# Moving a spatial product and a projection behind attention as three-part products, and input products into attention

## The chip, the core and the metric

The kernel runs on one core of one Trainium2 chip. Its engines work on queues of their own and meet at semaphores: TensorE (PE) for matrix products, with weight loads (PEld) that overlap them, the vector engine (DVE), the scalar engine (ACT), GpSimd (POOL) and SyncE (SP), which issues most DMAs. The metric is the device time of one execution in microseconds; lower is better.

## The reference

Three layers follow one another, for 2 batches of 576 positions, 8 heads of 64, model width 512:

```python
# 1. attention that keeps the 32 largest scores of each row
scores = scale * q @ k.T
kth    = 32nd largest of each row
attn   = softmax(where(scores >= kth, scores, -1e9))
x      = concat_heads(attn @ v)
# 2. gated MLP with a product over positions ("spatial")
h      = gelu(x @ w_in);  u, v = halves of h           # 512 columns each
v_n    = layernorm(v) * g_ln
v_s    = einsum('ts,bsd->btd', w_sg, v_n) + b_sg       # spatial product
x      = x + (u * v_s) @ w_out                         # projection
# 3. routed experts, one of 8 for each token
e      = argmax(x @ w_gate), or the expert of the token before if x @ w_local >= 0
out    = softmax(x @ w_gate)[e] * (relu(x @ w1[e]) @ w2[e])
```

## The kernel before

Positions are cut into tiles of 128; a batch has four whole tiles (j = 0 to 3) and one of 64 (j = 4), and the two 64s share the tile `BOTH`. Attention runs in 72 units. A unit is one head of one whole tile, or two heads of a half tile: scores (L325), copy to `s_sb` (L328), a search for the 32nd largest in eight segments (L354 to L371), sign and exponential (L365, L367), a mask (L378 to L381), five transposes (L393), copy `pt` (L396), product with v (L401). After four units the rows are divided into `row` (L406 to L417). Batch 0 takes its tiles in the order 0, 1, 2, 3, 4; batch 1 as 4, 0, 1, 2, 3. So `BOTH` is complete early in batch 1.

All other work is cut into steps that wait in a list, `between`. After each unit `pump` gives a credit of 2.0 to 2.4 us (`RATE`, L26) and takes steps off the list while the credit lasts; what is left when attention ends follows by itself. In program order the list holds:

- `load_mlp`: w_in in eight pieces (each two vector, two scalar and one GpSimd instruction, `from_double`), and w_sg;
- for each complete tile its `mlp_in`: x @ w_in in 16 products of 128 and 4 of 512 columns (L453, L459), GELU (L466, L468), layernorm, and `logits_x` (L566);
- once `BOTH` is queued: `spread(0)`, the first batch's spatial product, 40 products of 288 columns (L541); `load_projection` (w_out, and w_out times the router weights); `tail(0)`, which holds the first batch's logits and route (`decide`) and its projection, 16 products of 512 columns (L617);
- after attention `spread(1)` and `tail(1)`: logits, route, count, and the projection of batch 1 and of `BOTH`.

A plain product of float32 operands is issued as two instructions in the trace. In batch 1 the late products are written otherwise: each operand is split into a rounded half and a rest (`in_two`, an ACT copy and a subtraction on GpSimd or the vector engine), and `product` adds three instructions, high by high, high by rest, rest by high (L523). `parts` prepares the splits when `spread(1)` starts.

The order on each engine is made when the program is built, by a scheduler that follows priorities (`high_priority`) and fixed pairs (`issue_after`). The tiles that hold splits are taken from attention's rings of buffers (`s_sb` 7, `e_sb` 5, `q` or `qh` 3, `kk` 8, `v1` 2), so they also wait for units to be done.

After the last projection the rows are in DRAM (`xrows`). The addresses `frm` come from small products (L901), and 30 products of ones (L1017) keep TensorE at work until the gather (L926) brings the rows; the experts follow (L995, L1006), eight in a row.

Of the kernel before, what the change touches and what calls it, by code (L numbers as in the profile page):

```python
# [30 lines left out]
PLAIN = (True, True)  # L31

# [5 lines left out]
FILL = (2, 2, 2, 3)  # L38
# [6 lines left out]
def tile_topk_gmlp_moe(  # L45
# [123 lines left out]
    def attention(fast):  # L169
# [39 lines left out]
        def load_sg():  # L209
            nc.sync.dma_start(w_sg_sb[:, :NJ - 1, :], w_sgT[:(NJ - 1) * P].rearrange("(c p) t -> p c t", p=P))  # L210
            load_last(0)
# [34 lines left out]
        KK, QH, QL, V1, XB, XT, VN, UT, LG, DONE = {}, {}, {}, {}, {}, {}, {}, {}, {}, []  # L246

        def load_k(b, h):
            if PLAIN[b]:
                if h % 2 == 0:  # L250
                    KK[b, h] = kv.tile([P, S], F32R, name="kk", bufs=8).bitcast(F32)
                    nc.sync.dma_start(KK[b, h], kT[b, h:h + 2].rearrange("h d s -> (h d) s"))
                return
            kr = raw.tile([P, S], F32, name="kr")
            for s in range(2):
                nc.sync.dma_start(kr[s * D:(s + 1) * D], kT[b, h])
            KK[b, h] = kv.tile([P, S], F32R, name="kk", bufs=8)
            nc.scalar.activation(KK[b, h], kr, AF.Copy)
            nc.gpsimd.tensor_tensor(KK[b, h][D:], kr[D:], KK[b, h][D:].bitcast(F32), op=OP.subtract)
# [12 lines left out]
        def load_q(b, j, g):  # L272

            if PLAIN[b]:

                src = qT[b, g:g + 4].rearrange("(a h) d s -> (h d) a s", h=2)
                qr = kv.tile([P, 4, P], F32R, name="qh", bufs=3).bitcast(F32)
                if j < NJ - 1:
                    for s in range(2):
                        at = slice(s * D, (s + 1) * D)  # L280
                        nc.gpsimd.memset(qr[at, 1 - s::2, :], 0.0)
                        nc.sync.dma_start(qr[at, s::2, :], src[at, :, j * P:(j + 1) * P])
                    for h in range(4):
                        QH[b, j, g + h] = qr[:, h, :]
                    return
                nc.gpsimd.memset(qr[:, :2, :], 0.0)
                for s in range(2):
                    nc.sync.dma_start(qr[s * D:(s + 1) * D, :2, s * LAST:(s + 1) * LAST],
                                      src[s * D:(s + 1) * D, :, (NJ - 1) * P:])
                for a in range(2):  # L290
                    QH[b, j, g + 2 * a] = qr[:, a, :]
                return
            src = qT[b, g:g + 4].rearrange("h d s -> d h s")
            qr = raw.tile([P, 4, P], F32, name="qraw")
            if j < NJ - 1:
                for s in range(2):
                    nc.sync.dma_start(qr[s * D:(s + 1) * D], src[:, :, j * P:(j + 1) * P])
            else:
                nc.gpsimd.memset(qr, 0.0)
                for s in range(2):  # L300
                    for a in range(2):
                        nc.sync.dma_start(qr[s * D:(s + 1) * D, a::2, a * LAST:(a + 1) * LAST],
                                          src[:, a::2, (NJ - 1) * P:])
            qh = kv.tile([P, 4, P], F32R, name="qh", bufs=3)
            nc.scalar.activation(qh, qr, AF.Copy)
            ql = kv.tile([P, 4, P], F32R, name="ql", bufs=3)
            nc.gpsimd.tensor_tensor(ql, qr, qh.bitcast(F32), op=OP.subtract)
            for h in range(4):
                QH[b, j, g + h], QL[b, j, g + h] = qh[:, h, :], ql[:, h, :]
# [5 lines left out]
        def scores(b, j, i):  # L315

            s_ps = ps_s.tile([P, 2, 512], F32, name="s_ps")
            if PLAIN[b]:
                terms = [(QH[b, j, i], KK[b, i - i % 2]) if j < NJ - 1 else (QH[b, j, 2 * i], KK[b, 2 * i])]
            else:  # L320
                hs = [i] if j < NJ - 1 else [2 * i, 2 * i + 1]
                terms = [(w[b, j, h], KK[b, h]) for h in hs for w in (QH, QL)]
            for m, (w, k) in enumerate(terms):
                for n in range(2):
                    nc.tensor.matmul(s_ps[:, n, :HS], w, k[:, n * HS:(n + 1) * HS],  # L325
                                     start=m == 0, stop=m == len(terms) - 1)
# [115 lines left out]
        def mlp_in(t):  # L442
# [3 lines left out]
            def u(f):  # L446
                if f == 0:
                    if j == 0 or t == BOTH:
                        VN[b] = one.tile([P, 1 if t == BOTH else NJ - 1, F2], F32, name="vn2" if t == BOTH else "vn")
                        UT[b] = one.tile([P, CF, P if t == BOTH else FULL], F32, name="ut2" if t == BOTH else "ut")  # L450
# [32 lines left out]
        SG, VN2, UT2, OUT2, ORT2 = [], {}, {}, [], []  # L483
# [8 lines left out]

        def parts():
# [665 lines left out]
```

## Time and profile before

| | |
|---|---|
| three timed runs | 583.7, 582.37, 582.16 us; median 582.37 |
| the profiled execution | 582.34 us, of which the span in the trace is 580.5 |
| TensorE clock granted | 0.985 of full speed on average, 1.00 from 80 us to the last 40 |
| busy over the span | PE 90%, DVE 58%, ACT 51%, POOL 44% |
| attention, first unit's copy to last `pt` | 8.7 to 354 us |
| split products behind attention | 373.2 to 410.5 us |
| first gather for the experts | 414.6 us |

A share over the span mixes stretches with different limits: the experts (from 418 us) are TensorE and weight loads from DRAM alone, attention uses four engines. What a move is worth is read from the stretch that it leaves and the one that it enters. In the views below a product's duration runs from its issue to its modelled end; products overlap, so the pace is the distance of two starts.

### The profile page before, as it was taken

To read this page: it belongs to the slowest core of one execution; us is meant where nothing else is said; L and a number is where in the kernel's file an instruction comes from. 1 tells how busy PE (TensorE), PEld (TensorE's weight loads), DVE (VectorE), ACT (ScalarE), POOL (GpSimd) and SP (SyncE) were. 2 spreads that over 40 slices of the span, in tenths; PEclk is the share of its full clock that TensorE was granted. 3 is DMA by queue.
4 is the path that set the end of the run, shared out by engine and by line. 5 is a ranking of instruction groups with operands and counts; after the bars stand their busy time and mean duration, and the time that the engine had idled before them with its cause. 6 is when DMAs were issued, how large, how long until landed. Compare 5 with 4: busy or idle time off the path is not lost. (4 is left out here: it accounts for less than half of the span.)

```text
span 580.5 us, 10259 instructions
## 1 busy us (share of the span) xinstructions
PE 521.7 (90%) x3414; PEld 442.7 (76%) x3414; DVE 335.2 (58%) x1626; ACT 297.0 (51%) x545; POOL 258.0 (44%) x382
## 2 busy tenths in 40 slices
PE   6566898989989799998999999989889999999993
PEld 3445686867868587887866787786579999999992
DVE  4789998969789798689998711266301111111110
ACT  3579888979787887479877432321010111011110
POOL 5497997657758475447676510520310101000010
PEclk9799899999999999999999999999999999999997
DMA  8962320000000000003101300002599997684000
GB/s 173 268 191 81 112 72 5 25 1 28 20 10 28 19 16 5 11 20 92 46 29 36 110 20 19 0 1 74 186 356 387 389 376 264 234 297 169 18 36 17
DMA packets 42609, 61.55 MB, mean 106 GB/s; under 512 B 14056, under 2 KB 18152, under 8 KB 42544
## 3 DMA queue, kind: packets, MB, share of 16 engines
q1 hardware_dynamic: 40880, 55.80, 29.5%
q0 software_dynamic: 1664, 4.97, 2.5%
q8 instruction: 30, 0.49, 0.4%
q14 instruction: 35, 0.29, 0.2%
HBM read 53.68 MB, written 7.33 MB: 105 GB/s over the span
## 5 line engine op out<-in xcount | busy, mean ns | idle before, releaser
L401 PE MATMUL pv<-v,pt 128*128 128x128 f32 (+1 forms) x720 | 104.7, 279 | 7.3 <-DVE row L417 4.8
L401 PEld LDWEIGHTS pv<-v,pt 128*128 128x128 f32 x720 | 96.2, 194 | 15.1 <-DVE row L417 5.5
L369 POOL TENSOR_TENSOR rest<-s_sb,sg 128x576 f32<-128x576 f32 x72 | 93.3, 1296 | 28.5 <-ACT sg L365 27.2
L325 PE MATMUL s_ps<-kk,qh 128*128 128x288 f32 x288 | 86.2, 423 | 16.0 <-ACT s_sb L328 15.0
L354 DVE MAX8 cand<-s_sb 128x8 f32<-128x72 f32 x576 | 88.7, 219 | 13.7 <-ACT s_sb L328 13.5
L393 PE MATMUL pt_ps<-ident,e_sb 128*128 128x128 f32 x360 | 68.1, 277 | 16.3 <-ACT pt L396 5.5
L995 PE MATMUL h_ps<-xw,w_sb 128*128 128x152 f32 (+6 forms) x512 | 76.5, 298 | 1.0 <-DMA w_sb<-in_w_dram 1.0
L1006 PE MATMUL y_ps<-hT,w_sb 128*128 128x152 f32 (+6 forms) x512 | 75.3, 299 | 0.9 <-DMA w_sb<-in_w_dram 0.9
L325 PEld LDWEIGHTS s_ps<-kk,qh 128*128 128x128 f32 x288 | 50.2, 194 | 31.3 <-ACT s_sb L328 21.4
L995 PEld LDWEIGHTS h_ps<-xw,w_sb 128*128 128x128 f32 x512 | 71.4, 190 | 1.3 <-ACT hT L998 1.3
L1006 PEld LDWEIGHTS y_ps<-hT,w_sb 128*128 128x128 f32 x512 | 71.0, 190 | 1.2 <-DMA w_sb<-in_w_dram 1.2
L396 ACT ACTIVATE pt<-pt_ps 128x640 f32<-128x640 f32 x72 | 50.3, 699 | 36.3 <-PE pt_ps L393 36.1
L998 ACT ACTIVATE hT<-h_ps 128x152 f32<-128x152 f32 (+6 forms) x32 | 9.7, 302 | 113.1 <-PE h_ps L995 109.9
L393 PEld LDWEIGHTS pt_ps<-ident,e_sb 128*128 128x128 f32 x360 | 45.2, 143 | 28.2 <-ACT pt L396 8.3
L365 ACT ACTIVATE sg<-s_sb,last 128x576 bf16<-128x576 f32 x72 | 55.6, 773 | 18.7 <-DVE last L357 15.4
L371 DVE MAX8 next<-rest 128x8 f32<-128x583 f32 x72 | 54.7, 759 | 8.2 <-POOL rest L370 8.0
L367 ACT ACTIVATE e_sb<-s_sb,nm 128x576 f32<-128x576 f32 x72 | 55.5, 772 | 1.9 <-POOL nm L362 1.7
L967 POOL DMA_INDIRECT out_dram<-orow,to x10 | 10.0, 999 | 103.1 <-ACT orow L966 48.3
L328 ACT ACTIVATE s_sb<-s_ps 128x576 f32<-128x576 f32 x72 | 46.3, 642 | 13.3 <-PE s_ps L325 12.8
L1000 DVE TENSOR_SCALAR hT<-h_ps 128x152 f32<-128x152 f32 (+6 forms) x32 | 10.3, 323 | 73.6 <-PE h_ps L995 68.6
L379 POOL TENSOR_TENSOR e_sb<-e_sb,mask 128x576 f32<-128x576 f32 x36 | 46.3, 1287 | 13.4 <-ACT e_sb L367 6.7
L1008 DVE COPY yT<-y_ps 128x152 f32<-128x152 f32 (+6 forms) x32 | 9.9, 323 | 64.2 <-PE y_ps L1006 64.2
(247 smaller groups left out, 827.2 us busy)
## 6 DMA issues: line engine op xcount, KB each, us to landing
w_sb<-in_w_dram SPq DMA_DIRECT2D x32, 1024.0 KB, 12.4
dbl<-in_w_in_dram SPq DMA_DIRECT2D x8, 512.0 KB, 4.5
kk<-in_kT_dram SPq DMA_DIRECT2D x8, 288.0 KB, 4.9
qh<-in_qT_dram SPq DMA_DIRECT2D x32, 64.0 KB, 2.4
v<-in_v_dram SPq DMA_DIRECT2D x8, 256.0 KB, 6.1
dbl<-in_w_out_dram SPq DMA_DIRECT2D x4, 512.0 KB, 3.7
xin<-row SPq DMA_DIRECT2D x8, 256.0 KB, 2.0
back<-xin SPq DMA_DIRECT2D x8, 256.0 KB, 2.6
```

What stands on the lines that cost most here:

```text
L325: nc.tensor.matmul(s_ps[:, n, :HS], w, k[:, n * HS:(n + 1) * HS], start=m == 0, stop=m == len(terms) - 1)
L328: EVACS.append(nc.scalar.activation(s_sb.rearrange("p (n s) -> p n s", n=2), s_ps[:, :, :HS], AF.Copy))
L354: nc.vector.max(cand[:, 8 * g:8 * g + 8], s_sb[:, g * w:(g + 1) * w])
L365: nc.scalar.activation(sg, s_sb, AF.Sign, bias=last8[:, un, 7:8], scale=-LESS, accum_out=cnt)
L367: nc.scalar.activation(e_sb, s_sb, AF.Exp, bias=nm, scale=scale)
L369: nc.gpsimd.tensor_tensor(below[:, :S], s_sb, sg, op=OP.mult)
L371: nc.vector.max(next8[:, un, :], below)
L393: tr = nc.tensor.transpose(pt_ps[:, t * P:(t + 1) * P], p_sb[:, k0:k0 + P], ident)
L396: nc.scalar.activation(pt.rearrange("p t q -> p (t q)"), pt_ps[:, :NJ * P], AF.Relu)
L401: nc.tensor.matmul(PV[b][:, i % g, :], pt[:, t, :], V1[b][:, t, w * i * (D + 1):w * i * (D + 1) + nv], start=t == 0, stop=t == NJ - 1)
L995: nc.tensor.matmul(hp[:, :W], w1_sb[:, c, f * P:(f + 1) * P], xw[:, c, at], start=c == 0, stop=c == CD - 1)
L1006: nc.tensor.matmul(yp[:, :W], w2_sb[:, f, c * P:(c + 1) * P], hT[:, f, :W], start=f == 0, stop=f == CE - 1)
```

## The change

- `spread(0)` and the projection of batch 0 leave the list within attention. The list now holds `load_projection` right after `BOTH`, then the `mlp_in` of batch 1's tiles as they complete. After attention one list follows: `spread(0)`, logits and route of batch 0, `spread(1)`, logits, route and count of batch 1, and the projection of all nine tiles, `BOTH` last.
- `spread(0)`, the first logits and the projection of batch 0 are split products too: three instructions for each, on splits of w_sg, `vn`, `u` and w_out.
- The splits are prepared in three calls: `parts` (w_sg, `vn` of batch 0; subtractions of `vn` on the vector engine), `parts_late` (`vn` of batch 1), `parts_out` (w_out). The last 64 rows of w_sg for batch 1 go to a buffer of their own, loaded by `load_last`.
- `vn` and `ut` get a buffer for each batch; the `kk` ring has 6 instead of 8; a path that was not used (`PLAIN` false) is taken out.

```diff
-FILL = (2, 2, 2, 3)
+FILL = ((3, 5, 4), (2, 4, 3, 3))
...
-        def load_last(b):
+        def load_last(w, b):
             half = [slice(a * LAST, (a + 1) * LAST) for a in range(2)]
-            nc.gpsimd.memset(w_sg_sb[half[1 - b], NJ - 1, :], 0.0)
-            nc.sync.dma_start(w_sg_sb[half[b], NJ - 1, :], w_sgT[FULL:])
+            nc.gpsimd.memset(w[half[1 - b]], 0.0)
+            nc.sync.dma_start(w[half[b]], w_sgT[FULL:])
...
+        def split_spatial():
+            for j, hi in enumerate(of_values(S)):
+                SG[0, j] = SG[1, j] = (hi, of_scores())
+
         def parts():
...
+            split_spatial()
+            last = of_rest()
+            load_last(last, 1)
+            SG[1, NJ - 1] = (of_rest().bitcast(F32R), of_rest().bitcast(F32R))
+            rooms = [of_scores, of_scores] + [of_weights] * 5 + [of_queries] * 3
+            for j in SPREAD[0]:
+                VN2[j if j == NJ - 1 else (0, j)] = hi, lo = rooms.pop(0)()[:, :F2], rooms.pop(0)()[:, :F2]
+                in_two((hi, lo), vn_of(0, j), nc.vector)
+                in_two(SG[0, j], w_sg_sb[:, j], nc.gpsimd)
+            in_two(SG[1, NJ - 1], last, nc.gpsimd)
...
+        def parts_late():
+            sg = wts.tile([P, NJ, S], F32, name="w_sg_sb").bitcast(F32R)
+            rooms = of_values(F2) + [sg[:, j, :F2] for j in range(NJ)]
+            for j in SPREAD[1]:
+                if j < NJ - 1:
+                    VN2[1, j] = (rooms.pop(0), rooms.pop(0))
+                    in_two(VN2[1, j], vn_of(1, j), nc.gpsimd)
+            rooms += [kv.tile([P, S], F32, name="kk", bufs=6).bitcast(F32R)[:, :F2] for _ in range(6)]
+            for f in range(CF):
+                UT2[1, f] = (rooms.pop(0), rooms.pop(0))
+
+        def parts_out():
+            rooms = [of_weights] * 5 + [of_queries] * 3
+            for f in range(CF):
+                OUT2.append((rooms.pop(0)(), rooms.pop(0)()))
+                in_two(OUT2[f], w_out_sb[:, f], nc.gpsimd)
...
-                if b == B - 1:
-                    if j == js[0] and f == 0 and n == 0:
-                        parts()
-                    product(ps[0], part(VN2[j], slice(None), slice(f * P, (f + 1) * P)), part(SG[j], slice(None), at),
-                            j == js[0], j == js[-1])
-                else:
-                    nc.tensor.matmul(ps[0], vn_of(b, j)[:, f * P:(f + 1) * P], w_sg_sb[:, j, at], start=j == js[0],
-                                     stop=j == js[-1])
+                if j == js[0] and f == 0 and n == 0:
+                    (parts, parts_late)[b]()
+                if b == B - 1 and f == 1 and n == 0 and j == js[0]:
+                    parts_out()
+                vn = VN2[j if j == NJ - 1 else (b, j)]
+                product(ps[0], part(vn, slice(None), slice(f * P, (f + 1) * P)), part(SG[b, j], slice(None), at),
+                        j == js[0], j == js[-1])
...
-                else:
-                    nc.tensor.matmul(ps[0], u, w_out_sb[:, f, :], start=f == 0, stop=f == CF - 1)
+                product(ps[0], w, OUT2[f], f == 0, f == CF - 1)
...
+            steps = [step for t in [(b, j) for b in range(B) for j in range(NJ - 1)] + [BOTH] for step in project(t)]
+            return spread(0) + [(4.4, partial(decide, 0))] + spread(1) + [(4.4, partial(finish, 1, steps))]
...
                 if j == NJ - 1 and b == B - 1:
-                    between.extend(spread(0))
                     between.extend(load_projection())
-                    between.extend(tail(0))
             if b == B - 1:
-                between.extend(spread(b))
-                between.extend(tail(b))
+                between.extend(tail())
```

How the built order moves is shown at three places. A row is one instruction or several alike (xN), with its line, output and inputs; line numbers of the change are its own (scores L289, transposes L357, product with v L365, `mlp_in` L418 and L424, `logits_x` L564).

TensorE early in batch 1, before the change, where `mlp_in` of `BOTH` ends (L566):

```order
L566 MATMUL m_ps<-w_rt_sb,xT 128x90 x2
L541 MATMUL m_ps<-w_sg_sb,vn 128x288 x6
L401 MATMUL pv<-v_1852,pt 128x128
L393 MATMUL pt_ps<-ident,e_sb 128x128
L401 MATMUL pv<-v_1852,pt 128x128
L393 MATMUL pt_ps<-ident,e_sb 128x128
```

The same place with the change:

```order
L564 MATMUL m_ps<-w_rt_sb,xT 128x90 x3
L357 MATMUL pt_ps<-ident,e_sb 128x128 x5
L289 MATMUL s_ps<-kk,q 128x288 x2
L357 MATMUL pt_ps<-ident,e_sb 128x128 x5
L365 MATMUL pv<-v_1852,pt 128x128 x10
L289 MATMUL s_ps<-kk,q 128x288 x2
L365 MATMUL pv<-v_1852,pt 128x128 x5
L357 MATMUL pt_ps<-ident,e_sb 128x128 x5
L289 MATMUL s_ps<-kk,q 128x288 x2
L230 MATMUL m_ps<-ident,w_out_sb 128x128 x4
```

The products of `spread(0)` are gone from here, and three units pass before `load_projection` (L230) gives TensorE something else. At this point 54 units have their scores and 45 are transposed, in both orders.

TensorE at the end of attention, with the change (L403 transposes `row`):

```order
L365 MATMUL pv<-v_1852,pt 128x128 x9
L403 MATMUL m_ps<-ident,row 128x128 x2
L418 MATMUL m_ps<-xT,w_in_sb 128x128 x16
L424 MATMUL m_ps<-w_in_sb,xT 128x512 x4
L564 MATMUL m_ps<-w_rt_sb,xT 128x90 x4
L523 MATMUL m_ps<-v_4461,s_sb 128x288
```

The last tile's `mlp_in` directly follows the last product with v, and the first split spatial product (L523) follows it; before, the same `mlp_in` stood behind two others.

The vector engine at the hand-over to the experts, before (`back` is the last projection's sum, L620):

```order
L887 TENSOR_TENSOR slot_at_h<-iota_c,slot_h 128x100
L620 TENSOR_TENSOR back<-m_ps,back 128x512
L897 TENSOR_TENSOR idf_at<-slot_at_h,tokid 128x200
L897 TENSOR_TENSOR pslot_at<-slot_at_h,pparts 128x300
L620 TENSOR_TENSOR back<-m_ps,back 128x512
L903 TENSOR_REDUCE idf<-a_ps 128x10
```

and with the change (the sum is L610):

```order
L868 TENSOR_TENSOR slot_at_h<-iota_c,slot_h 128x100
L610 TENSOR_TENSOR back<-m_ps,back 128x512
L878 TENSOR_TENSOR idf_at<-slot_at_h,tokid 128x200
L878 TENSOR_TENSOR pslot_at<-slot_at_h,pparts 128x300
L884 TENSOR_REDUCE idf<-a_ps 128x10
```

The last sum moved ahead of `idf_at`. On TensorE the 20 products that read `idf_at` and `pslot_at` stood ahead of all 30 products of ones; with the change 20 of the 30 (L998) stand ahead of them (L882) and 10 behind.

## Rows read from the trace of the kernel before

**Rows 1.** Stretches: busy us (instructions) of each engine, clock, DMA.
```profile
core 0: us, PE busy (x) PEld busy (x) DVE busy (x) ACT busy (x) POOL busy (x), PEclk, DMA share, GB/s
98.60:176.20 77.60, 69.52 (x460) 57.61 (x459) 65.38 (x345) 65.35 (x115) 51.14 (x79) 1.00 0.07 20
227.00:373.20 146.20, 142.72 (x884) 113.26 (x883) 99.40 (x442) 88.42 (x157) 73.38 (x93) 1.00 0.11 38
260.00:300.00 40.00, 36.93 (x256) 30.86 (x255) 37.72 (x188) 35.51 (x67) 28.95 (x40) 1.00 0.17 54
373.20:410.50 37.30, 35.27 (x228) 29.44 (x227) 23.95 (x94) 6.77 (x17) 6.79 (x6) 1.00 0.12 37
```

**Rows 2.** TensorE in order of time: start us, us, engine, line, instruction.
```profile
227.16 3.11 PE L541 MATMUL m_ps<-w_sg_sb,vn 128*128 128x288 f32 x12
...
232.74 4.53 PE L541 MATMUL m_ps<-w_sg_sb,vn 128*128 128x288 f32 x18
237.11 0.49 PE L393 MATMUL pt_ps<-ident,e_sb 128*128 128x128 f32 x3
...
364.36 3.73 PE L453 MATMUL m_ps<-xT,w_in_sb 128*128 128x128 f32 x32
...
371.36 2.04 PE L566 MATMUL m_ps<-w_rt_sb,xT 128*128 128x90 f32 x16
373.19 0.38 PE L523 MATMUL m_ps<-s_sb,e_sb 128*128 128x288 f32 x1
...
381.01 0.40 PE L523 MATMUL m_ps<-s_sb,e_sb 128*128 128x288 f32 x1 [1.64 <-DVE ut L551]
...
391.03 0.40 PE L523 MATMUL m_ps<-kk,ort_h 128*9 128x512 f32 x1
...
394.18 0.47 PE L523 MATMUL m_ps<-kk 128*128 128x512 f32 x1
...
404.92 0.40 PE L523 MATMUL m_ps<-kk 128*128 128x512 f32 x1
...
410.49 0.41 PE L901 MATMUL a_ps<-idf_at,slot_at_l 128*128 128x20 bf16 x10
...
411.43 6.63 PE L1017 MATMUL y_ps<-slot_at_l,ones 128*128 128x512 bf16 x30 [0.27 <-DVE back L620]
```

**Rows 3.** Vector engine and GpSimd in order of time, at the hand-over.
```profile
410.68 0.69 DVE L620 TENSOR_TENSOR back<-m_ps,back 128x512 f32<-128x512 f32 x1 [0.87 <-PE m_ps L523]
...
411.50 0.17 DVE L919 TENSOR_SCALAR frm<-idf 128x10 int32<-128x10 f32 x1
...
414.55 1.24 POOL L926 DMA_INDIRECT xr<-xrows,frm  x1 [3.33 <-issue]
```

**Rows 4.** TensorE by line, 227 to 373: busy us, mean ns, idle before.
```profile
L541 PE MATMUL m_ps<-w_sg_sb,vn 128*128 128x288 f32 x80 | 20.6, 406 | 0.0
...
L617 PE MATMUL m_ps<-w_out_sb,ut 128*128 128x512 f32 x32 | 15.0, 602 | 0.0
...
L587 PE MATMUL m_ps<-ut,w_ort_sb 128*9 128x512 f32 x8 | 3.8, 593 | 0.0
...
L587 PE MATMUL m_ps<-ut,w_ort_sb 128*9 128x64 f32 x8 | 0.8, 220 | 0.0
```

**Rows 5.** By line over the span: the division and the copy.
```profile
L417 DVE TENSOR_TENSOR row<-pv,rc 128x256 f32<-128x256 f32 x16 | 6.6, 413 | 0.1
...
L440 ACT ACTIVATE xT<-m_ps 128x512 f32<-128x512 f32 x9 | 5.4, 599 | 5.8 <-PE m_ps L439 5.8
```

**Rows 6.** Scalar engine by line, 227 to 410.5.
```profile
L396 ACT ACTIVATE pt<-pt_ps 128x640 f32<-128x640 f32 x27 | 18.9, 699 | 29.2 <-PE pt_ps L393 29.2
...
L490 ACT ACTIVATE s_sb<-w_sg_sb 128x576 fp32r<-128x576 f32 x5 | 3.2, 677 | 0.4 <-DVE e_sb L381 0.4
```

**Rows 7.** Scalar engine in order of time: GELU of tiles 1 and 3, batch 0.
```profile
125.07 0.60 ACT L466 ACTIVATE row<-m_ps 128x512 f32<-128x512 f32 x1
...
193.79 0.60 ACT L466 ACTIVATE row<-m_ps 128x512 f32<-128x512 f32 x1
```

More of the change, by code (lines that the diff above doesn't have):

```diff
@@ L272, in load_q @@
         def load_q(b, j, g):
[L274 to L292, printed above, removed]
@@ L298, in load_q @@
             else:
-                nc.gpsimd.memset(qr, 0.0)
+                nc.gpsimd.memset(q[:, :2, :], 0.0)
                 for s in range(2):
[L301 to L306, printed above, removed]
@@ L317, in scores @@
             s_ps = ps_s.tile([P, 2, 512], F32, name="s_ps")
-            if PLAIN[b]:
-                terms = [(QH[b, j, i], KK[b, i - i % 2]) if j < NJ - 1 else (QH[b, j, 2 * i], KK[b, 2 * i])]
-            else:
[L321 to L326, printed above, removed]
+            h, pair = (i, i - i % 2) if j < NJ - 1 else (2 * i, 2 * i)
+            for n in range(2):
+                nc.tensor.matmul(s_ps[:, n, :HS], QH[b, j, h], KK[b, pair][:, n * HS:(n + 1) * HS], start=True,
+                                 stop=True)
             s_sb = wk.tile([P, S], F32, name="s_sb", bufs=7)
@@ new lines, in of_scores, with of_weights, of_rest, of_queries @@
+        def of_scores():
+            return wk.tile([P, S], F32, name="s_sb", bufs=7).bitcast(F32R)
+        def of_weights():
+            return wk.tile([P, S], F32, name="e_sb", bufs=5).bitcast(F32R)[:, :F2]
+        def of_rest():
+            return wk.tile([P, S + ADD], F32, name="rest", bufs=3)[:, :S]
+        def of_queries():
+            return kv.tile([P, 4, P], F32, name="q", bufs=3).bitcast(F32R).rearrange("p h q -> p (h q)")
+        def of_values(n):
+            room = kv.tile([P, NJ, V1[0].shape[2]], F32, name="v1").bitcast(F32R).rearrange("p j n -> p (j n)")
+            return [room[:, k * n:(k + 1) * n] for k in range(NJ)]
@@ L582, in logits @@
                 for c in range(CF):
[L583 to L588 removed]
+                    x = part(UT2[b, c], slice(None), at) if n > LAST else part(UT2[BOTH], slice(None), c, both)
+                    lm = product(ps[:E + 1, :n], part(ORT2, slice(None), c), x, c == 0, c == CF - 1)
                 ORDER.append(lm)
@@ L688, in count, with tail @@
             ORDER.append(mm)
-        def tail(b):
-            tiles = [(b, j) for j in range(NJ - 1)]
-            if b == B - 1:
-                tiles.insert(2, BOTH)
-            steps = [step for t in tiles for step in project(t)]
-            if b < B - 1:
-                return [(4.4, partial(decide, b))] + steps
-            return [(4.4, partial(finish, b, steps))]
+        def tail():
+            steps = [step for t in [(b, j) for b in range(B) for j in range(NJ - 1)] + [BOTH] for step in project(t)]
+            return spread(0) + [(4.4, partial(decide, 0))] + spread(1) + [(4.4, partial(finish, 1, steps))]
         def decide(b):
@@ L701, in spare @@
                 return ps_m.tile(shape, F32, name="m_ps")
-            if b < B - 1:
-                load_last(b + 1)
-            fills = list(FILL)
+            fills = list(FILL[b])
             def fill():
```

87 lines of the change are left out of this document (28 added, 59 removed).

## The prediction, made before the change was run

> **What bounds the kernel now.** I read the stretches first. From 227 to 373 us, where the second batch's attention runs and the first batch's late work is mixed in, TensorE is busy 142.7 of 146.2 us (97.6%), the vector engine 99.4 and the scalar engine 88.4 [rows 1]. In the first batch, where only `mlp_in` is mixed in (98.6 to 176.2 us), all three lie closer together: TensorE 89.6%, vector and scalar engine 84% each [rows 1]. So attention itself has no single bound; TensorE becomes one when it is given more. From 373 to 410.5 us, behind attention, TensorE does nearly everything (35.3 of 37.3 us; the scalar engine 6.8), and the last projection ends at 410.49 [rows 1, 2]. Then the rows of x go to DRAM, are gathered at 414.55 [rows 3], and the experts follow. I take the experts to be unchanged: what they cost is set by when the gather starts. So the sum is made at two marks: the last projection (E, 410.5 now) and the gather (E + 4.1 now).
>
> **What leaves attention.** `spread(0)` at L541 (20.6 us busy), the first batch's projection at L617 (15.0) and its logits at L587 (3.8 + 0.8): 40.2 us [rows 4]. 142.7 − 40.2 = 102.5 us of TensorE work stay ahead of the tail. The four `mlp_in` of the second batch are in that number on both sides, since already now they stand ahead of `spread(1)`; the change only moves three of them from the end of attention, where they fill it, into its middle.
>
> **How long those 102.5 us take.** The last `mlp_in`, of tile (1, 3), can't start before attention's last unit. It takes 7.0 us for its products (364.36 to 371.36) and half of 2.04 for its logits: 8.0 [rows 2]. Ahead of it lies a chain in which TensorE has nothing to do, since no step stands there in the new order: division, `row` (0.41), transposes, the copy `xT` (0.60) [rows 5], and, ahead of that copy on the scalar engine, three splits of `vn`. I put this at 2.2 us, an estimate from the two durations (1.0 together) and as much for the short steps and hand-overs; bounds 1 and 3.
> The other 94.5 us run beside 27 units of attention [rows 6]. Now TensorE waits 3.5 us in this stretch. With so much filler gone it will wait more. Two rows show how much: where weights are loaded and little else fills (260 to 300) its share is 92.3%, beside `mlp_in` 89.6% [rows 1]. Some 8 of the 27 units will run beside `load_projection`, 19 beside `mlp_in`: 90.4% on average, so 94.5 / 0.904 = 104.5 us. The ends: 97.6% as now (96.8 us), and the first batch's pace of two tiles of eight units in 68.7 us [rows 7], 27 × 4.29 = 115.9 us.
> One cost is moved earlier: the five splits of `w_sg` on the scalar engine (3.2 us now, late in attention, where it waits 29 us for transposes [rows 6]) stand, after, in one row in the first batch's attention, ahead of the fourth tile's GELU. Between 0 and 3.2; I take 1.5, since the engine is busy 84% there. The splits of `w_out` go the other way and lie beside the second spatial product; I count them at nothing, covered by its 16 us of TensorE time.
> The spatial product (0) can then start at 227.2 + 104.5 + 1.5 + 2.2 + 8.0 = 343.4 us; `spread(1)` starts at 373.19 now [rows 2].
>
> **What is added behind attention.** A split product of 288 columns is issued each 0.1336 us (75 from 381.01 to 391.03), one of 512 each 0.232 (24 from 404.92 to 410.49) [rows 2]. So 120 of the first are 16.0 us, 48 of the second 11.1, the 24 products of the first logits 3.2 (391.03 to 394.18), and the small transposes of the first batch's route about 1: 31.3. Gone is the wait of 1.64 ahead of 381.01, which came from a late `vn` of tile (1, 3). Tail: 37.3 + 31.3 − 1.6 = 67.0 us; E = 343.4 + 67.0 = 410.4, that is 0.1 earlier than now. The three-part form saves little: the 80 passes at L541 are issued each 0.243 us (18 from 232.74 to 237.11) [rows 2], 19.4 us against 16.0. The vector engine must drain two spreads in a row with a route inside the second; it is busy 24.0 of 37.3 us there now [rows 1], so I take no wait for it and keep 2 us for the range. The new `load_last` and its memset, the longer row of `back` loads on SP and the smaller `kk` ring have slack of several units or of a 2.8 us tile, and are taken at nothing; if a `kk` load is late after all, the start of the second batch slips with it.
> The Trainium skill's page "FP8 and Floating Point Precision" (TensorE Precision Notes) says that a true FP32 product is four passes through the array. Three of four would make the 19.4 us 14.6. The rows give 16.0, so the saving is 17% and not 25%; by the page the spatial term, and with it the forecast, would be 1.4 us lower.
>
> **The hand-over to the experts.** In the new order of TensorE 20 of the 30 idle products stand ahead of the small products that give `frm`, the gather's addresses; now all 30 stand behind them. And `idf_at` on the vector engine stands behind the last `back`, now ahead of it. An idle product is 0.22 us (6.63 for 30) and they start when the last `back` is done, E + 0.9 now (410.68 + 0.69) [rows 2, 3]. So `frm` is ready at E + 0.9 + 4.4 + about 0.9 = E + 6.2, where now it is at E + 1.2 and the gather waits for the rows until E + 4.1 [rows 3]. The gather is the later by 2.2 us; bounds 1.4 (idle products start at E) and 3.
>
> **Sum.** −0.1 + 2.2 = +2.1 us. The profiled execution took 582.34 us (span 580.5 and 1.8 around it), and the median of the three runs is 582.37, so nothing is to be converted: 584.5 us.
>
> **Rivals.**
> 1. TensorE stays full (faster). The filler that is left is enough, because vector and scalar engine have run ahead of it, as they may with seven `s_sb` buffers. For it speaks the 97.6% of now, against it that this share stands where 40 us more filler were there. At 97.6% and no cost for the splits: E is 9.3 earlier, with the gather's 2.2 still paid 575.2. The point from which it decides is a share of 92.3%, at which the 94.5 us take 102.4 and the sum is zero; above it the change is faster.
> 2. Nothing changes (582.4): exactly that share, which the stretch of 260 to 300 shows [rows 1].
> 3. Attention runs at its own pace (clearly slower). If a unit takes 4.29 us whatever fills it, E is 11.3 later and the time 596. For it speaks that three `mlp_in` bring three GELUs, each with two table switches, into the stretch; against it that in the last ten units no scores are left to compute. The Trainium skill's page "Perfetto Trace Analysis" (Optimization Strategy) advises interleaving stretches that contend for different engines. The change takes 31 us of TensorE work out of such a mix and puts it where the scalar engine is busy 6.8 of 37.3 us [rows 1]. By that rule alone this rival holds; the 92.3% of 260 to 300 speak against.
> 4. The scheduler's order of the hand-over costs nothing because the rows in DRAM are later still: the forecast less 2.2, which is rival 2.
>
> **Chances.** The forecast's own case (584 to 590) 0.40; rival 1 0.26; rivals 2 and 4 together 0.21; rival 3 (above 590) 0.13. A difference of 0.3% (1.75 us) is what these runs can tell from none: faster 0.26, same 0.21, slower 0.53. The range leaves one in ten at each side: 577 reaches into rival 1, 592 into rival 3; the forecast's own range is 583.5 to 589.
>
> **What would show it.** First, the start of the first split spatial product, 343.4 us (338 and earlier speak for rival 1, 350 and later for rival 3), and TensorE's busy share between 227 and that mark. Second, from there to the last projection 67 us; much more says that the vector engine's drains hold it. Third, from the last projection to the first gather 6.3 us instead of 4.1, with idle products ahead of the address products. Fourth, from the first gather to the end as long as now (580.5 − 414.55, 166 us). If the experts' part differs by more than a microsecond, the step that I left out is the wrong one.

## The result, and the profile after

The changed kernel takes 589.94 us (median of 4 runs, 589.86 to 590.52), beside 582.65 us for the kernel before: ratio 1.0125, 95% interval 1.0107 to 1.0142. It is 7.3 us slower. The forecast was 584.5 in a range of 577 to 592: the sign and the range held, the size (+2.1 us) was too small by 5 us, and the time lies above the forecast's own range of 583.5 to 589. The profiled execution has a span of 588.1 us, 7.6 more than before. One of the twelve executions of kernel 10 below took 1209 us, which nothing here explains; its ratio is that of the other eleven.

The forecast named four marks. They are read from TensorE's and GpSimd's rows; the end of the last projection is the start of its last group of instructions and 0.232 us for each of them:

| mark, us | before | forecast | after |
|---|---|---|---|
| first split spatial product (0) | – | 343.4 | 345.89 |
| last projection done (E) | 410.49 | 410.4 | 412.86 |
| from the one to the other | – | 67.0 | 66.97 |
| first gather | 414.55 | E + 6.3 = 416.7 | 421.52 = E + 8.66 |
| gather to the end of the span | 165.95 | 166 | 166.58 |

So the tail is as forecast. Attention is 2.5 us late, the hand-over 2.4 more than the forecast had put on it, and the experts 0.6. Against before, E is 2.4 later, the hand-over 4.6 longer: 7.6 with the experts.

The stretches, which answer to [rows 1] (us, then busy us and instructions of PE, PEld, DVE, ACT, POOL, then clock, DMA):

```profile
227.00:300.00 73.00, 69.72 (x483) 59.39 (x482) 67.63 (x349) 64.44 (x116) 51.14 (x73) 1.00 0.12 39
300.00:345.90 45.90, 36.10 (x248) 30.92 (x248) 18.46 (x35) 20.12 (x32) 19.14 (x16) 0.93 0.03 13
345.90:415.00 69.10, 67.62 (x431) 57.15 (x432) 43.97 (x157) 14.16 (x37) 7.39 (x6) 1.00 0.17 54
```

The first two in the kernel before:

```profile
227.00:300.00 73.00, 69.93 (x439) 58.63 (x439) 63.20 (x299) 54.86 (x99) 43.52 (x61) 1.00 0.11 36
300.00:345.00 45.00, 44.59 (x262) 32.27 (x261) 31.28 (x126) 26.11 (x45) 23.82 (x26) 1.00 0.18 60
```

Up to 300 us TensorE is 95.5% busy, as before, although the 20.6 us of `spread(0)` are gone from there: the `mlp_in` of two tiles stands there now (64 instructions at L418, 16 at L424). Behind 300 us it is starved, at 79%, while the vector and scalar engine are busy less than half of the time. TensorE in order of time, which answers to [rows 2]; in brackets the wait ahead and what ended it:

```profile
305.85 0.74 PE L357 MATMUL pt_ps<-ident,e_sb 128*128 128x128 f32 x5 [1.49 <-ACT pt L360]
311.97 2.47 PE L365 MATMUL pv<-v,pt 128*128 128x128 f32 x10 [5.39 <-DVE row L381]
314.23 0.63 PE L403 MATMUL m_ps<-ident,row 128*128 128x128 f32 x2
...
337.93 3.84 PE L418 MATMUL m_ps<-xT,w_in_sb 128*128 128x128 f32 x32 [0.69 <-ACT xT L404]
...
345.89 0.40 PE L523 MATMUL m_ps<-v,s_sb 128*128 128x288 f32 x1
...
412.16 0.86 PE L523 MATMUL m_ps<-q,pt 128*128 128x512 f32 x3
414.27 4.48 PE L998 MATMUL y_ps<-slot_at_l,ones 128*128 128x512 bf16 x19 [1.25 <-DVE back L610]
418.58 0.40 PE L882 MATMUL a_ps<-idf_at,slot_at_l 128*128 128x20 bf16 x10
...
425.20 0.88 PE L938 MATMUL a_ps<-ident,xr 128*128 128x128 f32 x4 [3.80 <-issue]
```

One wait stands out: 5.39 us ahead of the products of a unit with v, ended by `row`. The products behind it (2.47 us for ten) take nearly twice the 1.28 that ten take elsewhere: TensorE's granted clock, 1.00 up to 308 us, fell within the wait, in which TensorE had nothing to do, and was 0.50, the lower of its two levels (1.2 GHz), from 310 to 316 us:

```profile
310.00:316.00 6.00, 4.03 (x19) 4.06 (x20) 3.11 (x6) 1.10 (x2) 3.90 (x3) 0.50 0.12 46
```

The vector engine shows what `row` stood behind:

```profile
300.39 1.28 DVE L1086 TENSOR_SCALAR fc<-cnts 128x72 int32<-128x72 f32 x1
...
303.33 3.78 DVE L1082 TENSOR_SCALAR fa<-next 128x72 f32<-128x72 f32 x1
307.15 0.28 DVE L1083 SCALAR_TENSOR_TENSOR fa<-last,fa 128x72 f32<-128x72 f32 x1
...
308.61 1.35 DVE L1089 TENSOR_SCALAR fc<-fc 128x72 int32<-128x72 int32 x1
309.89 0.15 DVE L370 TENSOR_SCALAR dn<-pv 128x4 f32<-128x4 f32 x1
310.00 1.23 DVE L1090 TENSOR_TENSOR fa<-fa,fc 128x72 f32<-128x72 f32 x1
...
311.41 0.41 DVE L381 TENSOR_TENSOR row<-pv,rc 128x256 f32<-128x256 f32 x1
```

`fa` and `fc` are the check of the search (was an exact repeat needed?), eight instructions that run as soon as the last unit is searched; their result is read only behind the experts. In the kernel before seven of them took 0.2 to 0.3 us each, at 327.8 to 329.9, and the eighth (`fc` from `cnts`) 0.77 at 320.9. Here they stand between the last units and take up to 3.78 us, while GpSimd works beside them:

```profile
303.03 1.27 POOL L343 TENSOR_TENSOR e_sb<-e_sb,mask 128x576 f32<-128x576 f32 x1
304.27 1.40 POOL L456 TENSOR_TENSOR s_sb<-w_sg_sb,v 128x576 fp32r<-128x576 f32 x1
305.62 1.41 POOL L456 TENSOR_TENSOR rest<-rest 128x576 fp32r<-128x576 f32 x1
308.52 1.40 POOL L456 TENSOR_TENSOR s_sb<-w_sg_sb,v 128x576 fp32r<-128x576 f32 x1 [1.48 <-DVE e_sb L345]
309.87 1.27 POOL L343 TENSOR_TENSOR e_sb<-e_sb,mask 128x576 f32<-128x576 f32 x1
...
420.50 0.36 POOL L993 MEMSET yT<- 128x4 f32 x9 [35.58 <-DMA xrows<-back]
421.52 1.24 POOL L907 DMA_INDIRECT xr<-xrows,frm  x1 [0.66 <-issue]
```

The end of each long check instruction (307.11, 309.96, 311.23) is within 0.1 us of the end of a GpSimd one (307.03, 309.92, 311.14).

The last two rows are the hand-over and answer to [rows 3]: what GpSimd waits for there is not `frm` but the landing of the last write of rows. On the vector engine and on SyncE's queue:

```profile
408.26 0.17 DVE L830 SCALAR_TENSOR_TENSOR key<-pos,iota_e 128x8 f32<-128x8 f32 x1
...
413.53 0.68 DVE L610 TENSOR_TENSOR back<-m_ps,back 128x512 f32<-128x512 f32 x1
...
419.23 0.17 DVE L900 TENSOR_SCALAR frm<-idf 128x10 int32<-128x10 f32 x1
```

```profile
413.06 0.32 SPq L612 DMA_DIRECT2D xrows<-back  x1
417.15 1.11 SPq L612 DMA_DIRECT2D xrows<-back  x2
```

```profile
L1009 SPq TENSOR_LOAD <-regs_i x8: 263/272/539, 411.7 to 416.5; - x8
```

The last sum is done at 414.2, but its rows are written only from 417.15. Between them SyncE loads the order of the experts into registers, eight times, from 411.7 to 417. These loads need `regs_i`, which follows from `key`. Before, `key` ran at 403.30, as soon as `pos` was there; now `pos` is there at 396.9 and `key` runs 11 us later. In the built program its wait is for a split product of tile (1, 3) that reads `w_sg_sb`; the last of these are issued from 407.30 on, and `key` follows at 408.26. The change puts the split of `u`'s first quarter into `w_sg_sb` (`UT2[1, 0]`), in the pool on whose memory the experts' tables are laid.

### The profile page after: what moved, and what is told of

It reads as the page before. It is cut to its first block, busy times and chain, and to the rows that moved or that the text cites. A ratio compares the mean times of both kernels' runs of the same rounds, so it can differ in the third digit from the quotient of the medians.

```text
span 588.1 us, 10456 instructions
## 1 busy us (share of the span) xinstructions
PE 519.8 (88%) x3477; PEld 450.8 (77%) x3478; DVE 349.1 (59%) x1643; ACT 307.8 (52%) x566; POOL 260.4 (44%) x382
## 5 line engine op out<-in xcount | busy, mean ns | idle before, releaser
L365 PE MATMUL pv<-v,pt 128*128 128x128 f32 (+1 forms) x720 | 101.6, 280 | 8.5 <-DVE row L381 7.1
L289 PE MATMUL s_ps<-kk,q 128*128 128x288 f32 x288 | 86.7, 424 | 21.1 <-ACT s_sb L292 20.2
L365 PEld LDWEIGHTS pv<-v,pt 128*128 128x128 f32 x720 | 94.1, 195 | 13.8 <-issue 6.3
L318 DVE MAX8 cand<-s_sb 128x8 f32<-128x72 f32 x576 | 90.0, 222 | 9.2 <-ACT s_sb L292 9.0
L289 PEld LDWEIGHTS s_ps<-kk,q 128*128 128x128 f32 x288 | 50.3, 194 | 37.3 <-ACT s_sb L292 26.8
L357 PE MATMUL pt_ps<-ident,e_sb 128*128 128x128 f32 x360 | 65.1, 281 | 15.5 <-ACT pt L360 8.5
L976 PE MATMUL h_ps<-xw,w_sb 128*128 128x152 f32 (+6 forms) x512 | 78.2, 302 | 0.0
L976 PEld LDWEIGHTS h_ps<-xw,w_sb 128*128 128x128 f32 x512 | 72.9, 192 | 0.4
L357 PEld LDWEIGHTS pt_ps<-ident,e_sb 128*128 128x128 f32 x360 | 44.4, 145 | 27.7 <-issue 6.3
```

The source lines that it names most:

```text
L289: nc.tensor.matmul(s_ps[:, n, :HS], QH[b, j, h], KK[b, pair][:, n * HS:(n + 1) * HS], start=True, stop=True)
L318: nc.vector.max(cand[:, 8 * g:8 * g + 8], s_sb[:, g * w:(g + 1) * w])
L357: tr = nc.tensor.transpose(pt_ps[:, t * P:(t + 1) * P], p_sb[:, k0:k0 + P], ident)
L365: nc.tensor.matmul(PV[b][:, i % g, :], pt[:, t, :], V1[b][:, t, w * i * (D + 1):w * i * (D + 1) + nv], start=t == 0, stop=t == NJ - 1)
L976: nc.tensor.matmul(hp[:, :W], w1_sb[:, c, f * P:(f + 1) * P], xw[:, c, at], start=c == 0, stop=c == CD - 1)
```

## The experiments

Each ratio is to the kernel before, timed on the same chip in the same comparison.

| kernel | ratio | 95% interval | first split product | E | gather |
|---|---|---|---|---|---|
| the change | 1.0125 | 1.0107 to 1.0142 | 345.89 | 412.86 | E + 8.66 |
| 1 check later | 1.0044 | 1.0027 to 1.0061 | 342.17 | 409.44 | E + 8.23 |
| 2 `UT2[1, 0]` elsewhere | 1.0068 | 1.0045 to 1.0091 | 346.73 | 414.32 | E + 7.52 |
| 3 addresses first | 1.0118 | 1.0095 to 1.0141 | 345.27 | 412.25 | E + 8.29 |
| 4 three moves | 0.9996 | 0.9979 to 1.0013 | 343.25 | 411.15 | E + 5.18 |
| 5 loads behind the rows | 1.0001 | 0.9976 to 1.0025 | 341.31 | 409.23 | E + 5.01 |
| 6 even filler | 1.0046 | 1.0022 to 1.0069 | 344.45 | 412.38 | E + 5.02 |
| 7 extra filler | 1.0315 | 1.0271 to 1.0358 | 360.21 | 428.08 | E + 5.63 |
| 8 splits on the vector engine | 1.0076 | 1.0050 to 1.0102 | 343.87 | 410.85 | E + 8.87 |
| 9 `load_projection` in the last tile | 1.0038 | 1.0017 to 1.0060 | 343.81 | 411.69 | E + 5.22 |
| 10 the same, a tile earlier | 1.0018 | 1.0001 to 1.0034 | 341.74 | 409.64 | E + 6.18 |
| 11 `BOTH` seventh | 0.9986 | 0.9966 to 1.0006 | 343.09 | 410.97 | E + 4.25 |

Kernels with the same order up to there (4, 5, 11) differ by up to 1.9 us in the first split product, and a mark is that of one execution, which can lie 2 us off its kernel's median (run 7: 600.11 us beside 602.38). So a single mark is good to one or two microseconds; the ratios rest on 4 to 12 executions each.

**1. The check later.** The vector engine's check is queued behind a drain of `spread(0)`.

```diff
+                    DRAINS.append(drain)          # each drain of a spatial product
...
-    nc.vector.tensor_scalar(fa, next8[:, :, 7], 1e-30, None, op0=OP.is_le)
+    with tc.issue_after(DRAINS[2].ins):
+        nc.vector.tensor_scalar(fa, next8[:, :, 7], 1e-30, None, op0=OP.is_le)
...
```

> The changed kernel with one thing moved: the vector engine's check of the search (the instructions on fa and fc, L1082 to L1092, 10 of them) is queued behind the third drain of spread(0) instead of between the last units. Theory A (the check stands ahead of row and of masks on the vector engine at 303 to 311 us, TensorE waits 5.4 us for row, and runs at the lower clock for some 4 us after it): the wait of 5.4 us is gone, the first split spatial product starts at 338 to 340 us instead of 345.9, and the time falls by 6 to 8 us, to 582 to 584. Theory B (the last units have their own chain and nothing fills TensorE; the check only fills a hole): the wait moves to other releasers, the first split product stays within 2 us, time 588 to 590. Theory C (the splits of w_sg on GpSimd, queued ahead of masks, hold the last units): half of the wait stays, time 586 to 588.

TensorE at the same place:

```profile
306.17 0.74 PE L357 MATMUL pt_ps<-ident,e_sb 128*128 128x128 f32 x5 [1.38 <-ACT pt L360]
308.85 2.47 PE L365 MATMUL pv<-v,pt 128*128 128x128 f32 x10 [1.94 <-DVE row L381]
...
342.17 0.40 PE L523 MATMUL m_ps<-v,s_sb 128*128 128x288 f32 x1
```

The wait of 5.39 is 1.94, the first split product 3.7 us earlier, the time 0.81% (4.7 us) lower. B is out. A is right that the check costs, but the gain is two thirds of what it said, since 1.94 us of the wait and the lower clock behind it stay (0.53 from 309 to 312 us). What stays fits theory C. The vector engine, then GpSimd:

```profile
303.67 4.29 DVE L345 SCALAR_TENSOR_TENSOR e_sb<-s_sb,next,e_sb 128x576 f32<-128x576 f32 x1
...
308.28 0.42 DVE L381 TENSOR_TENSOR row<-pv,rc 128x256 f32<-128x256 f32 x1
```

```profile
304.59 1.40 POOL L456 TENSOR_TENSOR s_sb<-w_sg_sb,v 128x576 fp32r<-128x576 f32 x1
305.94 1.40 POOL L456 TENSOR_TENSOR rest<-rest 128x576 fp32r<-128x576 f32 x1
```

In the place where L1082 took 3.78 us, the mask L345 now takes 4.29 instead of 0.8, beside GpSimd's mask and the same two splits. So these 3.78 us were not the check's own price: whatever stands there waits. What the move saves lies behind it, where `row` no longer stands behind L1089 and L1090.

**8. The splits on the vector engine.** Whether GpSimd is what stretches the check.

```diff
-                in_two(SG[0, j], w_sg_sb[:, j], nc.gpsimd)
+                in_two(SG[0, j], w_sg_sb[:, j], nc.vector)
```

> The changed kernel with the five rests of w_sg subtracted on the vector engine instead of GpSimd; the check of the search stays where it is. Theory A (vector instructions of the check are held while a GpSimd instruction runs beside them: 1.2 to 3.8 us each instead of 0.2): they take 0.15 to 0.3 us each, the ten of them about 2.5 us instead of 8.1; the five subtractions add some 4 us to the vector engine but do not stand ahead of row; time 2 to 4 us lower than the changed kernel, 586 to 588. Theory B (the durations belong to the instructions): they stay as long, and the time is 590 to 593.

```profile
303.93 2.40 DVE L1082 TENSOR_SCALAR fa<-next 128x72 f32<-128x72 f32 x1
...
309.40 0.20 DVE L1089 TENSOR_SCALAR fc<-fc 128x72 int32<-128x72 int32 x1
...
309.85 0.22 DVE L1090 TENSOR_TENSOR fa<-fa,fc 128x72 f32<-128x72 f32 x1
```

Where no split stands beside them any more, L1089 and L1090 take 0.20 and 0.22 us instead of 1.35 and 1.23. L1082 still runs beside a mask and the one split that is left on GpSimd (303.63 to 306.25) and takes 2.40. So the durations belong to the neighbour, not to the instruction. The eight take 5.0 us instead of 8.6, where theory A said 2.5; 0.49% (2.9 us) of the time comes back, as it said.

**3. The addresses first.** The forecast's own reason for the hand-over, alone.

```diff
         for m in range(KEEP):
+            with tc.issue_after(placed[-1].ins):  # the last address product
-            nc.tensor.matmul(idle, ones, ...)
+                nc.tensor.matmul(idle, ones, ...)
```

> The changed kernel with all 30 products of ones behind the 20 address products on TensorE; key and the register loads stay as late as they are. The forecast's reason (the idle products ahead of the address products set the gather): frm about 2.5 us after the last projection, the gather waits for the rows alone and starts 4.3 us after the last projection, time 585.6. Rival (the rows themselves are late, because register loads stand ahead of their last writes on SyncE): the last write is still issued 4.2 us after the last projection and lands 7 to 7.5 us after it; the gather gains 0.5 to 1.5 us only, time 588.4 to 589.4.

SyncE, then GpSimd:

```profile
416.31 1.11 SPq L612 DMA_DIRECT2D xrows<-back  x2
```

```profile
420.54 1.24 POOL L909 DMA_INDIRECT xr<-xrows,frm  x1 [36.22 <-issue]
```

`frm` is there at 414.75, E + 2.5, and helps nothing: the rows are written at E + 4.1 and the gather follows at E + 8.29. The rival is right. The idle products ahead of the addresses cost at most 0.4 us as long as the rows are later still.

**2. `UT2[1, 0]` elsewhere.** It goes to the free `dbl` ring, so that `key` has no reader to wait for.

```diff
+            del rooms[:2]                         # two quarters of w_sg_sb
+            pair = raw.tile([P, 2 * DM], U32, name="dbl", bufs=2).bitcast(F32R)
+            rooms[:0] = [pair[:, :F2], pair[:, F2:]]
             for f in range(CF):
                 UT2[1, f] = (rooms.pop(0), rooms.pop(0))
```

> The changed kernel with UT2[1, 0] (the split of the second batch's first quarter of u) in a buffer of the dbl ring instead of w_sg_sb. Theory A (the first step of the experts' preparation, key, waits for the memory of w_sg_sb, read last by the projection of tile (1, 3); behind it come the register loads on SyncE, which stand ahead of the last writes of rows, and the address products): key starts by 400 instead of 408.3, the last write of rows is issued within 1 us after the last sum instead of 3, the first gather is 4.0 to 4.6 us after the last projection instead of 8.7, time 589.9 - 4.3 = 585.6. Theory B (key is early or late without effect, since the idle products ahead of the address products set the gather): gather stays at 8 us or more, time 589 to 590.

`key` now runs at 400.65, the register loads are done at 409.7, the address products come before the last projection ends (412.09), and `frm` is there at 412.75. But the gather is at E + 7.52, against theory A: the last sum waits 3.59 us for the x rows of `BOTH`:

```profile
417.00 0.69 DVE L613 TENSOR_TENSOR back<-m_ps,back 128x512 f32<-128x512 f32 x1 [3.59 <-DMA back<-xin]
```

Their loads are issued from 411.07 to 412.2, as early before E (3.25 us) as in the change (3.16), but land 4.8 us later, where run 4's land in 2.3; why is open. The time is 0.57% (3.3 us) lower, more than the hand-over's 1.1 us. In this trace 2.3 us lie behind the gather (164.26 to the end of the span, 166.58 in the change): the idle products reach to within 1.05 us of the gathered rows and TensorE stays at its full clock (1.00 from 422 to 440 us). In the change TensorE has nothing to do for 3.80 us there, its clock is at the lower level (0.50) from 428 to 432 us, and the first 32 products of the experts take 7.91 us, where 24 take 4.71 here.

**4 and 5. Both causes away, then the register loads too.** The fourth kernel joins 1 and 2 and puts the memset of `yT` behind the fourth gather; the fifth adds:

```diff
+            with tc.issue_after(written[-1]):     # the last write of rows
-            er = nc.values_load(regs_i[0:1, r:r + 1], ...)
+                er = nc.values_load(regs_i[0:1, r:r + 1], ...)
```

> The changed kernel with the check of the search behind the third drain of spread(0), UT2[1, 0] in the dbl ring, and the memset of yT queued behind the fourth gather. If both causes are right and independent: 589.9 - 7 - 4.3 = 578.6 us, which is 4 us less than before the change. If the 7 us are not there (the last units are bound by their own chain), 585; if only the check counts, 583.

> The kernel of the run with three moves, and besides the eight register loads of the experts' order on SyncE are queued behind the last write of rows (before, they stood among the last loads of back and the last writes). Theory A (in the run with three moves the last sum waited 1.26 us for its x rows, whose load stood behind register loads, and TensorE's last products were done 2 us before it): the gather comes 4.0 to 4.5 us after the last projection and the time is 2 us lower than with three moves, some 0.35% below the kernel before the change. Theory B (what is taken from SyncE there is given back by the first weights, whose load now stands behind a register load): within 1 us of the run with three moves.

The fourth is 1.29% (7.5 us) below the change and level with the kernel before. 1 and 2 had given 4.7 and 3.3: within the intervals the two causes add. The 578.6 that I expected is missed, because the check was priced at 7 and the hand-over at 4.3. The memset's share is small: from the first of the last two writes to the gather it is 4.12 us here and 4.37 in the change. The last sum, in the fourth and in the fifth:

```profile
411.49 0.69 DVE L614 TENSOR_TENSOR back<-m_ps,back 128x512 f32<-128x512 f32 x1 [1.26 <-DMA back<-xin]
```

```profile
409.42 0.69 DVE L614 TENSOR_TENSOR back<-m_ps,back 128x512 f32<-128x512 f32 x1 [1.11 <-PE m_ps L526]
```

In the fifth it waits for TensorE alone, as theory A said, but the gather comes at E + 5.01 and not at E + 4.0 to 4.5: 0.17 us is gained. That it stands 2.1 us earlier in the trace (414.24) is the first split product, 1.9 us earlier in this execution and long before any of these loads. The ratio doesn't move; theory B holds.

**7. Extra filler.** 40 plain products of `spread(0)` once more inside attention, into a tile that nobody reads. It prices the work that was taken away.

```diff
+                    between.extend(extra())       # steps of plain products vn x w_sg
                     between.extend(load_projection())
```

> As the run with the loads behind the rows, and 40 plain products of spread(0) are computed once more inside attention, where they stood before the change, into a tile that nobody reads: 20.6 us of TensorE work (80 instructions issued each 0.243 us, 19.4 us). It measures what such work costs inside attention. Forecast's reading (TensorE at 90% without it, 97.6% with all of it): 40.2 us of work took 146.2 - 116.2 = 30 us there, so this half costs 13 to 16 us. If attention had room (other engines bound it): 8 us or less. If TensorE alone bounds it: 19 to 20 us, and the work is then better done behind attention in three parts (16.0 us).

The first split product is 18.9 us later than in 5 and the time 3.1% (18.3 us) higher, for 19.4 us of issue. The stretch where they stand:

```profile
227.00:260.00 33.00, 32.99 (x187) 27.44 (x186) 21.94 (x103) 19.24 (x35) 13.94 (x21) 1.00 0.05 15
260.00:300.00 40.00, 37.25 (x260) 31.75 (x259) 37.52 (x185) 31.94 (x60) 30.63 (x42) 1.00 0.17 55
300.00:345.00 45.00, 39.42 (x282) 33.24 (x280) 23.81 (x89) 31.70 (x48) 23.06 (x25) 1.00 0.03 10
```

Up to 260 us TensorE is full, the vector engine two thirds busy, and behind 300 us the waits are still there. Early in batch 1 TensorE has no room, and work costs its full time: in 5, without the extra products, TensorE is busy for 31.63 of the 33.00 us from 227 to 260, and the vector engine for 31.64: both are full there. My 13 to 16 us were wrong.

**6, 9, 10. Filler moved to the starved end.** 6 sets the credit of batch 1 to 1.5 us; 9 and 10 put `load_projection` first in the list at the last tile, or the one before.

```diff
-RATE = (2.0, 2.0, 2.0, 2.0, 2.0, 2.4, 2.4, 2.4, 2.2, 2.2)
+RATE = (2.0, 2.0, 2.0, 2.0, 2.0, 1.5, 1.5, 1.5, 1.5, 1.5)
```

```diff
-                if j == NJ - 1 and b == B - 1:
-                    between.extend(load_projection())
...
+                if b == B - 1 and m == NJ - 1:    # NJ - 2 in run 10
+                    between[:0] = load_projection()
```

> As the run with the loads behind the rows, and the credit of batch 1 is 1.5 us for a unit instead of 2.2 to 2.4, so that mlp_in lasts longer between the units. Theory A (TensorE has too much filler up to 300 us, 95% busy, and none behind it): its waits between 300 and 340 us shrink, the first split spatial product is 2 to 4 us earlier, the time 2 to 4 us lower. Theory B (the filler delays no unit where it stands; the last units are late because of their own chain): no change within 1 us. Theory C (mlp_in of tile (1, 2) is now left for after the last unit): 2 to 6 us slower.

> As the run with the loads behind the rows; load_projection (needs no tile of batch 1) is taken off its place behind BOTH, where TensorE is 95% busy, and stands first in the list when the last tile's units begin, where TensorE waits. Theory A (attention is bound by TensorE where filler is, and starved in its last ten units): its work leaves 230 to 260 us and fills waits after 300 us; the first split spatial product starts 3 to 6 us earlier than 341.3, the time falls by as much, to 577 to 580. Theory B (the last units' waits are short and in series, and steps that need vector and scalar engine there delay the units): no change within 1 us. Theory C (mlp_in of tile (1, 2) now follows load_projection and is left for after the last unit): 1 to 4 us slower.

> The same with load_projection first in the list when the units of the last tile but one begin. Theory A: as in the other, 3 to 5 us less than the run with the loads behind the rows. Theory B: no change. Theory C does not hold here, since mlp_in of tile (1, 2) comes later than load_projection in any case; if this one is faster than the other, the left-over mlp_in was what cost.

None is faster than 5 and theory A fails in all three. 6 and 9 are 0.4% slower, the size of theory C; in 9 the logits of two tiles instead of one are left for after the last unit (16 instructions at 342.05, 8 in 5); in 6 no such left-over shows, and its cause is open. 10 is level with 5 within the intervals.

**11. `BOTH` seventh of nine projections**, otherwise as 5.

```diff
-            ... [(b, j) for b in range(B) for j in range(NJ - 1)] + [BOTH] ...
+            ... [(0, 0), (0, 1), (0, 2), (0, 3), (1, 0), (1, 1), BOTH, (1, 2), (1, 3)] ...
```

> As the run with the loads behind the rows, and the projection takes BOTH as the seventh of nine tiles instead of the last, so that the last write of rows is one of 128 rows instead of two of 64. Theory A (the two writes are what makes the gather come 4.1 us after the last sum's end, where it was 3.2 before the change): 3.2 us again, time 0.9 us lower than with the loads behind the rows, 0.1 to 0.3% below the kernel before. Theory B (the 4.1 us have another cause): gather still 4.0 or more after the end of the last sum, no change.

```profile
415.22 1.24 POOL L911 DMA_INDIRECT xr<-xrows,frm  x1 [32.79 <-issue]
```

The last sum ends at 411.97, so the gather follows 3.25 us after it, as before the change (3.2) and not 4.1. Theory A's mechanism holds; the ratio 0.9986 includes 1. This is the best version, and it isn't shown to beat the kernel before.

## Why the forecast was right in sign and too small

- **The sign was luck for the most part.** The +2.1 was the hand-over's +2.2, for idle products ahead of the addresses. `frm` is ready about when forecast (419.40, E + 6.5; forecast E + 6.2), but the rows land later still (420.50), so that these products cost at most 0.4 (run 3). What made the change slower, the check and the late writes of rows, stands nowhere in the sum.
- **The exchange itself was right.** Without the check the first split product comes at 341.3 to 343.25 us (runs 1, 4, 5, 11), where 343.4 was forecast, and the tail is 66.97 us where 67.0 was (67.9 in 4, 5 and 11). With both side effects away the change costs nothing: 0.9986 to 1.0001. The move takes 40.2 us of products out of attention and brings the end of attention forward by 30 to 32; the tail grows by 30 to 31.
- **The share of 90.4%** came out by luck of a sum (97.42 of 108.70 us from 227.00 to 335.70, 89.6%). TensorE was 95.5% busy to 300 us and 79% behind it (with the check), because two of the `mlp_in` that are left stand ahead of 300 us, where TensorE could not take more (run 7). That nothing is ready for it in the last ten units, whose scores are done by 290.6, is argued; moving filler there gained nothing (6, 9, 10). The forecast spread one share over all 27 units.
- **The step that failed first** is the one left out: the check of the search. I took nothing but the splits and `load_projection` to be moved relative to the last units. Without `spread(0)` and the projection the vector engine comes to the check while units still need it and while GpSimd splits `w_sg`. It costs 3.7 us at the first split product; run 1 gives 4.7 us of time. The 3.78 us of L1082 are not in that: the mask that stands there instead is held as long.
- **The splits of `w_sg`** were priced on the scalar engine (1.5), a term that no run isolates. What shows is their other half on GpSimd, which holds the vector engine: 2.9 us of time with the check in place (run 8), and the wait of 1.94 that is left without it (run 1). A kernel with both the check and the splits out of the way was not run, so that what the splits cost alone is open.
- **The hand-over** was +2.2 for the idle products ahead of the addresses; it is +4.6, and not for that reason (run 3). The step "the gather waits for `frm`" failed: it waits for rows, whose last writes come at E + 4.29 (0.91 before). They stand behind register loads, and these behind a `key` that waits for memory: in the change and in 1, 3 and 8, which leave `key` late, they are issued 0.1 to 0.2 us behind the last of these loads, and with `key` early they come at E + 1.06 (run 4). Run 2 alone doesn't show it, since its x rows land late. Another 0.9 us is that two writes of 64 rows come last instead of one of 128 (run 11). I had followed the order of TensorE and the vector engine past this place and not SyncE's queue, nor whose memory the experts' tables lie on.
- **Three parts**: 120 products from 345.89 to 361.84 are 0.133 us each, the 16.0 us of the rows. The Trainium skill's page "FP8 and Floating Point Precision" (TensorE Precision Notes) gives a true FP32 product four passes; the estimate from it, three quarters of 19.4, was 14.6, and the trace does not agree.
- **Rivals.** Rival 1 and 2 are out for the change as it is: the first split product is not at 338, and equality came back only when the side effects were removed; then rival 2's share holds too (run 5: 96.28 of 104.10 us from 227.00 to 331.10, 92.5%). Rival 4's mechanism is there (run 3), but not its time, since the rows were later than it took them to be. Rival 3's price (596) is not reached, nor its mechanism: work in the mix was not cheap, for in run 7 19.4 us of it moved the first split product by 18.9 us. The Trainium skill's page "Perfetto Trace Analysis" (Optimization Strategy) says that interleaving regimes with different most-contended engines may help; run 7 does not show that gain here.

## What to carry to other kernels

When work leaves a busy stretch, ask not only what gets the time but what is next in each queue: an instruction that nobody needs soon may now stand ahead of one that is waited for. When it is moved away, look again: what stands in its place may be held by the same neighbour. When tiles are given other buffers, look which later pool lies on that memory and who there has to wait for the new reader. Follow every queue at a hand-over, the one that loads registers included, and price filler by adding some: one run told what it cost where it stood.

## What the runs showed of the hardware that was not expected

Some vector instructions wait for GpSimd. The kernel before has it too; first the vector engine, then GpSimd:

```profile
323.99 1.29 DVE L664 TENSOR_TENSOR oh<-eid,coded 128x40 bf16<-128x40 int32 x1
...
327.82 0.21 DVE L1101 TENSOR_SCALAR fa<-next 128x72 f32<-128x72 f32 x1
```

```profile
323.82 1.41 POOL L491 TENSOR_TENSOR v<-w_sg_sb,s_sb 128x576 fp32r<-128x576 f32 x1
325.94 1.28 POOL L379 TENSOR_TENSOR e_sb<-e_sb,mask 128x576 f32<-128x576 f32 x1 [0.72 <-ACT e_sb L367]
```

L664, on 40 columns, ends with the GpSimd instruction beside it; L1101, with GpSimd idle from 327.2, takes 0.21 us, and the same instruction 3.78 in the change. It need not be a small one: the mask L345 of run 1 took 4.29 us. MAX8 instructions in the same stretches keep their 0.76 us, and `dn` and `row` of the change, which read products of TensorE, their 0.15 and 0.41 us, with GpSimd at work beside them (309.89 and 311.41). The Trainium skill's page "SBUF — State Buffer" (Who interferes with whom) states it: vector instructions with two inputs from SBUF, or in a mode that uses two ports, share a pair of ports with GpSimd, and the one that comes second is blocked until the first is done. The traces agree, with one addition: L1082 of the change started at 303.33 and did not get in when the GpSimd instruction that ran then ended at 304.30, nor at 305.67, but at 307.03, when GpSimd had no next one ready.

A register load on SyncE is not free for the DMAs queued behind it: eight take from 411.7 to 417 us, 0.66 us each with the check of the value.
